# Attention and two MLPs on one core: raw weights fetched earlier and converted from the chunk's first step

## The chip, the core and the metric

The kernel runs on one core of a Trainium2 chip. The metric is the device time of one execution in microseconds (us). Before the change it is 1036.7 us, the median of 3 runs (1035.36 to 1037.4). The core's engines work side by side, each through its own instructions in order, and wait for each other by semaphores: TensorE (PE, with its weight loads PEld), VectorE (DVE), ScalarE (ACT), GpSimd (POOL) and SyncE (SP), which issues the DMAs.

## The reference

```python
def _attn_ref(q, k, v, w1, b1, w2):          # q, k, v: [4, 8, 576, 64]
    ...
    scores = scale * np.matmul(q, k.transpose(0, 1, 3, 2)) + bias.transpose(2, 0, 1)[None, :, :, :]
    ...
    return np.matmul(attn, v)                # attn: softmax of the scores

def _moe_ref(x, w_in, w_out):                # x: [2304, 512], w_in: [512, 2048], w_out: [2048, 512]
    h = x @ w_in
    g = h - np.tanh(h)
    return g @ w_out

def _moe2_ref(x, w_in, w_out, s, b):
    h = x @ w_in
    r = np.maximum(h, 0.0)
    return (s * (r * r) + b) @ w_out

def reference(**kwargs):
    ...
    return _moe2_ref(x=_moe_ref(x=x, **moe_kwargs), **moe2_kwargs)   # x: attn_out as 2304 tokens
```

The weights of both MLPs come as 64-bit floats, so the kernel has to turn each into 32-bit ones, in two parts (a rounded one and what it leaves), before TensorE can use them.

## The kernel before, in words

The program is written in the order in which each engine runs it; no scheduler changes it. Attention goes over 16 pairs of heads in 80 periods (numbered n, with a tail to n = 85). Then comes the **chunk** (`CHUNKS`): 512 tokens of the first MLP with its 16 slices f of the hidden dimension, one per step n = 0 to 15. Then come the super-blocks (`SUPER`), where a product is made of 7 smaller ones: unit sums of the tokens (`tokens`, made in pieces that stand in `xq`) times sums of the weights (`load_w`, `combine`, `part`). The block has 8 pairs p of slices.

A step n of the chunk issues `gemm1(n)` (12 matmuls, h = x times the slice's w_in), `gate(n)` (tanh on ACT, a subtraction on DVE) and `gemm2(n - 2)` (12 matmuls with the slice's w_out); `split(n - 1)` (ACT rounds g, DVE takes the rest) stands ahead of `gemm1(n)`. h lies in one of two PSUM buffers, so `gemm1(n)` writes the one that `split(n - 2)` was the last to read. The products of slices 0 and 1 are made in attention's tail (`PR`).

Between these stands the **conversion** of the 32 half slices of weights, numbered k in the order of the list `wq`: (f, 0) is slice f of w_in, (f, 1) of w_out. `fetch(k)` brings 512 KB of raw weights; conversion k is then `begin(k)` (POOL takes the sign, ACT the value y), `high(k)` and `low(k)` (two DVE operations, the second writes the 32-bit weight x) and `both(k)` (ACT rounds x, POOL takes the rest, and a DMA writes x to `win_d` when it is a w_in, or the two parts to `wsp_d` when it is a w_out):

```python
    def begin(k, raw):
        ...
        x, sg = place(f"s{(0, 1, 6)[k % 3] if k < 32 else (0, 1, 6, 4, 5)[k % 5]}", [512]), place(f"s{2 + k % 2}", [512])
        y = ypool[0].tile([128, 512], F32, tag="y", name="y") if ypool else x
    ...
    def weights_tick():
        a, b_, c = wdone
        if c < b_:
            both(c)
            wdone[2] += 1
        if b_ < a:
            high(b_)
            low(b_)
            wdone[1] += 1
        if a in raw_w:
            begin(a, raw_w.pop(a))
            wdone[0] += 1
```

So x of conversion k lies in one of three buffers, and `low(k)` (line 155) waits until the DMA of `win_d` that reads x of conversion k - 3 has landed, where there is one. y has two PSUM buffers, so `begin(k)` on ACT (line 145) waits for `low(k - 2)`. A tick of the chunk is `both(c)`, `high` and `low` of c + 2 and `begin(c + 3)`. Attention converts k = 0 to 7 in its periods (`TK`), and issues 11 fetches (`FT`, k = 0 to 10); its tail begins conversions 8 to 10. At the chunk's start 8 are done. The number of finished conversions that a step wants is 8 + 2 (n - 2), so steps 0 and 1 have one tick each (a rule of their own), 2 and 3 none, and from step 4 on there are two in each. `fetch_more` then issues the fetches of up to 7 conversions ahead. All these DMAs go through SP, whose issues stand in program order.

Lines that the following speaks of: 372 `gemm1`, 380 and 381 `gate`, 388 and 389 `split`, 613 `gemm2`, 117 `fetch`, 144 and 145 `begin`, 150 `high`, 155 `low`, 161 and 100 `both`, 167 and 176 its DMAs, 775 and 778 the token units, 730 `combine`, 738 and 100 `part`, 920 the super-block's products.

Of the kernel before, what the change touches and what calls it, by code (L numbers as in the profile page):

```python
# [30 lines left out]
RATE = 2.0  # L31
# [13 lines left out]

FT = {1: 0, **{4 + 4 * k: k for k in range(1, 11)}}
ND = 8
TK = {}  # L50
for j, n in enumerate(sorted([41, *range(9, 80, 5)])):
# [15 lines left out]
def tile_kernel(ctx, tc, qk, vd, wcat, wts, sb, ltab, psib, ipsi8, out):  # L67
# [35 lines left out]
    wt, wc_t = {}, {}  # L103

    wq = [(0, 0), (1, 0), (0, 1), (2, 0), (1, 1), (3, 0), (2, 1), (3, 1), (4, 0)]
    wq += [(5 + j // 2 - j % 2, j % 2) for j in range(22)] + [(15, 1)]
    wx_t, wdone = {}, [0, 0, 0]

    raw_w = {}
# [68 lines left out]
# [13 lines that stand above are left out]
# [42 lines left out]
    with ExitStack() as c0:  # L233
# [62 lines left out]
        for n in range(NG + 2):  # L296
            if n < NG:
# [3 lines left out]
                for g in range(4 * G, 4 * G + 4):  # L301
                    hid = hids[g] = hp_.tile([128, LW], F32, tag="h", name="hid")
                    k = min(range(2), key=lambda k: held[k] + HC[k][0] + HC[k][1] * nd)
# [88 lines left out]
    with ExitStack() as ca:  # L392
# [15 lines left out]
        load, hi, lo = load_x(0)  # L408
# [190 lines left out]
    with ExitStack() as cb:  # L599
# [61 lines left out]
        j = 0  # L661
        for P in range(1, 16):
            q, p = divmod(P, 8)
# [47 lines left out]
        def load_w(q, p):  # L711
            if p >= NF // 2:
                q, p = q + 1, p - NF // 2
            if q < len(SUPER):
                if (q, p) not in wf_t:
                    wf_t[q, p] = place(f"w{4 - p}" if q == 0 and p < 2 else f"st{(p + 1) % 2}", [2, 512])
                nc.sync.dma_start(out=wf_t[q, p], in_=win_d[SUPER[q][0], 2 * p:2 * p + 2].rearrange("f p n -> p f n"))
# [37 lines left out]
        def tokens(q):  # L755

            layer, c0, hw = SUPER[q]
            kept = {}

            def raw(kk, half):  # L760
                return kept[kk][:, half * hw:half * hw + hw]

            def load(*kks):
                if q and 0 not in kept:
                    c = place(f"C{(q + 1) % 2}", [4096])
                    for kk in range(4):
                        kept[kk] = c[:, 2 * hw * kk:2 * hw * kk + 2 * hw]
                for kk in kks:
                    if not q:
                        kept[kk] = place(f"w{5 + kk}", [2 * hw])  # L770
                    nc.sync.dma_start(out=kept[kk], in_=source(layer, kk, c0, 2 * hw))

            def hi(u, *xs):
                for i, x in enumerate(xs):
                    nc.scalar.copy(unit(q, u, i, 0), x)

            def lo(u, i, x):
                nc.vector.tensor_tensor(out=unit(q, u, i, 1), in0=x, in1=unit(q, u, i, 0).bitcast(F32), op=ALU.subtract)  # L778

            def minus(o, a, b):  # L780
                nc.vector.tensor_tensor(out=o, in0=a, in1=b, op=ALU.subtract)

            def los(u, *xs):
                for i, x in enumerate(xs):
                    lo(u, i, x)

            def first(i):
                lo(0, i, raw(i, 0))
                minus(raw(i, 0), raw(i, 1), raw(i, 0))

            def third(i):
                minus(raw(i, 0), raw(2 + i, 0), raw(i, 0))
                minus(raw(i, 1), raw(2 + i, 1), raw(i, 1))

            def both(k, h):
                return [raw(k + i, h) for i in range(2)]

            return [lambda: load(0, 1), lambda: load(2, 3),
                    lambda: hi(0, *both(0, 0)), lambda: first(0), lambda: (first(1), hi(3, *both(0, 0))), lambda: los(3, *both(0, 0)),
                    lambda: ([minus(raw(i, 0), raw(2 + i, 1), raw(i, 0)) for i in range(2)], hi(1, *both(0, 0))),  # L800
                    lambda: los(1, *both(0, 0)), lambda: third(0), lambda: (third(1), hi(2, *both(0, 1))),
                    lambda: los(2, *both(0, 1)), lambda: hi(4, *both(2, 0)), lambda: (los(4, *both(2, 0)), hi(5, *both(0, 0))),
                    lambda: (los(5, *both(0, 0)), hi(6, *both(2, 1))), lambda: los(6, *both(2, 1))]

        g_at = {}

# [36 lines left out]
        xq = tokens(0)  # L843
        xq.insert(3, xq.pop(1))
        for n in range(NS):
            want = min(32, ND + max(0, int(RATE * (n - 2))))
            if n < 2:
                weights_tick()
            last = [seq[n - 1]] if len(PR) < n <= len(seq) else []
            if n > 12:  # L850
                split(*last.pop())
            while wdone[2] < want:
                weights_tick()
                if last:
                    split(*last.pop())
            if last:
                split(*last.pop())
            fetch_more(AHEAD)
            c, f = seq[n]
            if n >= len(PR):  # L860
                gemm1(c, f)
                gate(c, f)
            if n >= LAG:
                gemm2(*seq[n - LAG])
            for _ in range({8: 1, 9: 2, 10: 2, 11: 1, 12: 1, 13: 1, 14: 1, 15: 2}.get(n, 0)):
                xq.pop(0)()
            if n == 6:
                load_w(0, 0)
            if n == 9:
                combine(0, 0)  # L870
            if n == 11:
                part(0, 0)
                load_w(0, 1)
            if n == 14:
                combine(0, 1)
        flush(9)
        for _ in range(3):
            n, f, x, _ = back.pop(0)
# [1 line left out]
            wt[f, 1] = place(f"w{x}", [2, 512], F32R)  # L880
            nc.sync.dma_start(out=wt[f, 1].bitcast(F32), in_=wsp_d[f])
        split(*seq[-1])
        while len(xq) > 3:
            xq.pop(0)()

        h_ctx.close()
        ypool.clear()
# [6 lines left out]
        for q, (layer, c0, hw) in enumerate(SUPER):  # L894
# [30 lines left out]
            for p in range(NF // 2):  # L925
                keeps(q, p, "S")
                X, Y, Z, V = (bank(t, hw) for t in ("XYZV", "YXZV")[p % 2])
                load_w(q, p + 2)
                u2, r, t_x = (ring(F32)[:, 0:hw] for _ in range(3))
                product(X, p, 4, 0, True)  # L930
                nc.scalar.copy(u2, X)
                if p + 1 < NF // 2:
                    part(q, p + 1)
                product(Y, p, 0, 1, True)
                nc.vector.tensor_tensor(out=u2, in0=Y, in1=u2, op=ALU.add)
                product(Z, p, 1, 2, True)
                nc.vector.tensor_tensor(out=r, in0=Z, in1=u2, op=ALU.add)
                product(V, p, 2, 3, True)
                nc.vector.tensor_tensor(out=Y, in0=V, in1=r, op=ALU.add)  # L939
                if q == p == 0:  # L940
                    xq.pop(0)()
                if pend:
                    second_products(0, 2 * p - 2, pend.pop(0))
                elif fill:
                    fill.pop(0)()
                squashed(layer, Y, r)
                units(layer, held_unit(layer, 2 * p + 1), Y, r)
                if q == p == 0:
                    xq.pop(0)()
                    xq.pop(0)()  # L950
                keeps(q, p, "A")
                product(X, p, 5, 4, False)
                squashed(layer, X, t_x)
                units(layer, X, X, t_x)
                product(Z, p, 6, 5, False)
                nc.vector.tensor_tensor(out=Z, in0=Z, in1=u2, op=ALU.add)
                g1 = two(hw)
                upper(layer, X, g1)
                t_z = ring(F32)[:, 0:hw]
                squashed(layer, Z, t_z)  # L960
                lower(layer, X, g1)
                units(layer, Z, Z, t_z)
                product(V, p, 3, 6, False)
                nc.vector.tensor_tensor(out=V, in0=V, in1=u2, op=ALU.add)
                g2 = two(hw)
                upper(layer, Z, g2)
                lower(layer, Z, g2)
                squashed(layer, V, t_z)
                units(layer, held_unit(layer, 2 * p), V, t_z)
                if pend:  # L970
                    second_products(0, 2 * p - 1, pend.pop(0))
                elif fill:
                    fill.pop(0)()
                pend = [g1, g2]
                if p + 1 < NF // 2:
                    combine(q, p + 2)
                keeps(q, p, "E")
                if q == FIRST1 and p + 1 < NF // 2:
                    for f in (2 * p + 2, 2 * p + 3):
                        renewed(f)  # L980
                if p == NF // 2 - 1 and not final:
                    xq = tokens(q + 1)
                    for _ in range(3):
                        xq.pop(0)()
# [104 lines left out]
```

## Time and profile before

| | |
|---|---|
| median of 3 runs | 1036.7 us |
| the profiled execution | 1036.71 us, its span 1034.9 us |
| PE, PEld, DVE, ACT, POOL busy | 99%, 80%, 71%, 56%, 56% of the span |
| DMA | 170.47 MB, mean 165 GB/s |
| chain that ended last | PE 85%, DVE 4%, DMA 2%, POOL 2% |

The span runs from the first to the last instruction of the profiled execution; the time has 1.8 us around it. Attention lies at about 50 to 282 us of the span, the chunk's steps at about 280 to 358 us, and the super-blocks follow. Busy shares are means over all of these; what one stage costs is read from that stage.

### The profile page before, as it was taken

The numbers are of one execution on the slowest core, as the hardware profiler recorded it, in microseconds if no ns is written. First come the engines' busy times: TensorE is split into PE (matmuls) and PEld (weight loads), VectorE is DVE, ScalarE is ACT, GpSimd is POOL, SyncE is SP. The second block draws the span as 40 slices with busy tenths as digits, with TensorE's granted clock in tenths as the row PEclk, the third lists the DMA queues.
The fourth block names the chain that finished last, engine by engine and source line by source line (L and its number), as shares of the span: only waits on it lengthen the run. The fifth ranks groups of instructions, "written<-read, shape, count | busy, mean of one in ns | idle before, by whom it ended". The sixth has DMA issues, their size and how long they took to land.

```text
span 1034.9 us, 18742 instructions
## 1 busy us (share of the span) xinstructions
PE 1023.1 (99%) x6664; PEld 832.1 (80%) x6664; DVE 738.3 (71%) x1495; ACT 584.1 (56%) x1208; POOL 577.6 (56%) x706
## 2 busy tenths in 40 slices
PE   9999999999999999999999999999999999999998
PEld 4366666666688789999788888999989998899986
DVE  8899999998668787887777776455575556655551
ACT  8887778777556565544545444455544444454441
POOL 3266666677558678850776631498515664076400
PEclk9999999999999999999999999999999999999999
DMA  7857666554199667867677548411202112031000
GB/s 282 321 178 243 202 214 206 175 176 124 58 360 337 256 223 269 279 218 253 214 242 246 203 146 313 132 62 41 90 23 92 41 61 92 1 96 58 1 31 30
DMA packets 68348, 170.47 MB, mean 165 GB/s; under 512 B 7456, under 2 KB 13728, under 8 KB 68256
## 3 DMA queue, kind: packets, MB, share of 16 engines
q1 hardware_dynamic: 67824, 168.89, 47.2%
q8 instruction: 52, 0.85, 0.3%
q10 hardware_dynamic: 432, 0.39, 0.1%
q14 instruction: 40, 0.33, 0.1%
HBM read 123.22 MB, written 46.04 MB: 164 GB/s over the span
## 4 chain that ended last, share of the span: by engine, by line
PE 85%; DVE 4%; DMA 2%; POOL 2%; ACT 1%; issue 1%; SPq 0%; DVEq 0%; ACTq 0%; POOLq 0%
PE a L613 22%; PE o L536 8%; PE Z L920 8%; PE V L920 8%; PE s L437 7%; PE Y L920 6%; PE X L920 5%; PE V L613 5%; PE Z L613 5%; PE t L481 3%; PE h L372 2%; PE X L613 2%; PE Y L613 2%; PE c L481 1%; DMA w<-x_d 1%
## 5 line engine op out<-in xcount | busy, mean ns | idle before, releaser
L100 POOL TENSOR_TENSOR C<-st,C 128x512 fp32r<-128x512 f32 x76 | 76.4, 1028 | 172.1 <-ACT C L738 133.0
L475 POOL TENSOR_SCALAR pn<-p,sm 128x576 f32<-128x576 f32 (+2 forms) x224 | 132.6, 609 | 61.6 <-DVE sm L466 36.0
L613 PE MATMUL a<-w,ring 128*128 128x512 f32 x576 | 146.5, 392 | 0.0
L613 PE MATMUL a<-ring,w 128*128 128x512 f32 (+1 forms) x576 | 127.5, 371 | 0.0
L613 PEld LDWEIGHTS a<-w,ring 128*128 128x128 f32 x576 | 107.5, 188 | 20.5
L613 PEld LDWEIGHTS a<-ring,w 128*128 128x128 f32 x576 | 105.5, 188 | 14.9
L458 ACT ACTIVATE p<-raw,mn 128x576 f32<-128x576 f32 x144 | 110.9, 773 | 5.0 <-DVE mn L444 2.2
L100 POOL TENSOR_TENSOR C<-XB,C 128x512 fp32r<-128x512 f32 x80 | 108.3, 1376 | 0.0
L444 DVE CUSTOM_DVE_ANT_0 raw<-s,bias 128x576 f32<-128x576 f32 x144 | 103.6, 751 | 4.8 <-PE s L437 4.3
L920 PE MATMUL Z<-C,C 128*128 128x384 f32 (+1 forms) x480 | 102.6, 347 | 1.9 <-DVE C L778 0.8
L536 PE MATMUL o<-pt,vv 128*64 128x256 f32 (+1 forms) x640 | 95.0, 418 | 0.3 <-DVE xo L543 0.2
L437 PE MATMUL s<-qk 64*128 64x288 f32 (+1 forms) x640 | 91.5, 429 | 1.0 <-DVE mn L444 1.0
L920 PEld LDWEIGHTS Z<-C,C 128*128 128x128 f32 x480 | 85.2, 188 | 8.2 <-DVE C L778 2.1
L437 PEld LDWEIGHTS s<-qk 64*128 64x128 f32 (+1 forms) x640 | 47.0, 175 | 41.4 <-issue 18.3
L144 POOL TENSOR_SCALAR s<-w 128x512 f32<-128x512 f32 x60 | 48.2, 807 | 51.9 <-DVE s L150 25.4
L730 POOL TENSOR_TENSOR XB<-st 128x256 f32<-128x256 f32 x76 | 61.3, 807 | 14.5 <-DMA st<-win_d 12.3
L519 ACT COPY pt<-t 128x512 f32<-128x512 f32 x64 | 37.3, 583 | 44.5 <-PE c L481 29.5
L815 ACT ACTIVATE ring<-Y 128x384 f32<-128x384 f32 (+1 forms) x40 | 20.5, 513 | 73.9 <-PE Y L920 42.2
L815 ACT ACTIVATE ring<-X 128x384 f32<-128x384 f32 (+1 forms) x40 | 20.5, 513 | 71.0 <-DVE X L939 37.2
L481 PEld LDWEIGHTS t<-ident,pn 64*128 64x128 f32 x1184 | 51.7, 139 | 7.6 <-issue 0.6
L536 PEld LDWEIGHTS o<-pt,vv 128*64 128x64 f32 x640 | 38.9, 136 | 22.9 <-DVE xo L543 0.5
L481 PE MATMUL t<-ident,pn 64*128 64x64 f32 x1184 | 54.2, 223 | 0.0
(167 smaller groups left out, 2270.1 us busy)
## 6 DMA issues: line engine op xcount, KB each, us to landing
w<-in_wts SPq DMA_DIRECT2D x60, 512.0 KB, 4.8
w<-wsp_d SPq DMA_DIRECT2D x47, 512.0 KB, 4.9
st<-win_d SPq DMA_DIRECT2D x38, 512.0 KB, 3.9
qk<-in_qk SPq DMA_DIRECT2D x16, 864.0 KB, 6.1
bias_d<-m SPq DMA_DIRECT2D x36, 296.0 KB, 4.0
bias<-bias_d SPq DMA_DIRECT2D x32, 288.0 KB, 5.0
win_d<-s SPq DMA_DIRECT2D x32, 256.0 KB, 5.9
wsp_d<-w SPq DMA_DIRECT2D x16, 512.0 KB, 7.0
```

Source lines behind the costliest of these rows:

```text
L100: nc.gpsimd.tensor_tensor(out=lo, in0=raw, in1=hi.bitcast(F32), op=ALU.subtract)
L144: nc.gpsimd.tensor_scalar(out=sg, in0=hw, scalar1=0.0, scalar2=1.0, op0=ALU.mult, op1=ALU.mult)
L437: nc.tensor.matmul(o[0:n, c, 0:288], q[h, ee, t * 128:t * 128 + n], kk[h, ee], start=True, stop=True)
L444: nc.vector.tensor_tensor_reduce(out=raw.rearrange("p (c j) -> p c j", c=2), in0=s_t.pop((x, j))[:, :, 0:288], in1=bias_t[pairs[i][0], k]. ...
L458: nc.scalar.activation(out=p, in_=raw, func=AF.Exp, scale=-1.0, bias=mn, accum_out=sm[:, j:j + 1])
L475: nc.gpsimd.tensor_scalar(out=pn[:, c:c + b - a], in0=p[:, a:b], scalar1=sm[:, j:j + 1], scalar2=0.0, op0=ALU.mult, op1=ALU.add)
L481: nc.tensor.transpose(out_, in_, ident[ROWS[r], ROWS[r]])
L536: nc.tensor.matmul(o[h], v[:, e, j], unit_t[i, u][:, 8 if j == 4 else 4 * e + j, 0:n], start=(j == 0), stop=(j == 4))
L613: nc.tensor.matmul(o, x, y, start=first and j == 0, stop=last and j == 2)
L730: nc.gpsimd.tensor_tensor(out=o, in0=a, in1=b, op=op)
L815: nc.scalar.activation(out=t, in_=c, func=(AF.Tanh, AF.Relu)[layer])
L920: nc.tensor.matmul(o, cs[:, a, l, i * 128:i * 128 + 128], unit(q, u, i, r), start=begins and i == 0 and j == 0, stop=i == 1 and j == 2, sk ...
```

## The change

The list of the half slices gets another order from the tenth on: w_out of slices 4 to 7 first, then w_in of 6 to 9, then in turns again. Attention fetches three more raws (k = 11, 12, 13) at periods 60, 64 and 68. The chunk's wanted number becomes 8 + max(1, 2 n): one tick in steps 0 and 1, two in each of steps 2 to 12, none after. The token pieces (one more, since one was cut in two) all stand in steps 8 to 15, most of them in 12 to 15; before, four of them stood behind the loop and in the super-block's first pair. `combine(0, 0)` moves from step 9 to 11 and `part(0, 0)` from 11 to 13.

```diff
-FT = {1: 0, **{4 + 4 * k: k for k in range(1, 11)}}
+FT = {1: 0, **{4 + 4 * k: k for k in range(1, 11)}, 60: 11, 64: 12, 68: 13}
...
-    wq += [(5 + j // 2 - j % 2, j % 2) for j in range(22)] + [(15, 1)]
+    wq += [(5, 0), (4, 1), (5, 1), (6, 1), (7, 1), (6, 0), (7, 0), (8, 0), (9, 0)]
+    wq += [(8 + j // 2 + j % 2 * 2, 1 - j % 2) for j in range(12)] + [(14, 1), (15, 1)]
...
-                    lambda: los(2, *both(0, 1)), lambda: hi(4, *both(2, 0)), lambda: (los(4, *both(2, 0)), hi(5, *both(0, 0))),
-                    lambda: (los(5, *both(0, 0)), hi(6, *both(2, 1))), lambda: los(6, *both(2, 1))]
+                    lambda: los(2, *both(0, 1)), lambda: hi(4, *both(2, 0)), lambda: los(4, *both(2, 0)),
+                    lambda: (hi(5, *both(0, 0)), hi(6, *both(2, 1))), lambda: los(5, *both(0, 0)), lambda: los(6, *both(2, 1))]
...
-            want = min(32, ND + max(0, int(RATE * (n - 2))))
-            if n < 2:
-                weights_tick()
+            want = min(32, ND + max(1, int(RATE * n)))
...
-            for _ in range({8: 1, 9: 2, 10: 2, 11: 1, 12: 1, 13: 1, 14: 1, 15: 2}.get(n, 0)):
+            for _ in range({8: 1, 9: 2, 10: 1, 11: 1, 12: 2, 13: 3, 14: 3, 15: 3}.get(n, 0)):
...
-            if n == 9:
+            if n == 11:
                 combine(0, 0)
-            if n == 11:
+                load_w(0, 1)
+            if n == 13:
                 part(0, 0)
-                load_w(0, 1)
...
-        while len(xq) > 3:
-            xq.pop(0)()
...
-                if q == p == 0:
-                    xq.pop(0)()
...
-                if q == p == 0:
-                    xq.pop(0)()
-                    xq.pop(0)()
```

**SP at the chunk's start.** The rows `in_wts` are fetches, `wsp_d<-w` and `win_d<-s` are outputs of conversions; `win_d<-s_5025` before and `win_d<-s_5031` in the change are the same one, of conversion 9. Before:

```order
L176 DMA wsp_d<-w_4474 128x1024
L167 DMA win_d<-s_4995 128x512
L117 DMA w_5076<-in_wts 128x512
L117 DMA w_5078<-in_wts 128x512
L117 DMA w_5080<-in_wts 128x512
L117 DMA w_5082<-in_wts 128x512
L117 DMA w_5084<-in_wts 128x512
L117 DMA w_5086<-in_wts 128x512
L117 DMA w_5088<-in_wts 128x512
L176 DMA wsp_d<-w_4968 128x1024
L167 DMA win_d<-s_5025 128x512
```

And SP in the change, at the same place (its lines are one higher):

```order
L177 DMA wsp_d<-w_4480 128x1024
L168 DMA win_d<-s_5001 128x512
L118 DMA w_5087<-in_wts 128x512
L118 DMA w_5089<-in_wts 128x512
L118 DMA w_5091<-in_wts 128x512
L118 DMA w_5093<-in_wts 128x512
L177 DMA wsp_d<-w_4974 128x1024
L168 DMA win_d<-s_5031 128x512
L118 DMA w_5106<-in_wts 128x512
```

Four fetches in place of seven stand ahead of the output of conversion 9.

**DVE at the chunk's start.** `h<-h,ring` is a gate's subtraction, `ring<-h,ring` a split's; the pairs `y<-y,s` and `s<-w,y` are `high` and `low`. Before, from `low(10)` on (`s_5170` is written by `low(12)`, in the buffer of `s_5025`):

```order
L155 SCALAR_TENSOR_TENSOR s_5048<-w_3069,y 128x512
L381 TENSOR_TENSOR h<-h,ring 128x512
L389 TENSOR_TENSOR ring<-h,ring 128x512
L381 TENSOR_TENSOR h<-h,ring 128x512
L150 SCALAR_TENSOR_TENSOR y<-y,s_5095 128x512
L155 SCALAR_TENSOR_TENSOR s_5094<-w_5076,y 128x512
L389 TENSOR_TENSOR ring<-h,ring 128x512
L150 SCALAR_TENSOR_TENSOR y<-y,s_5171 128x512
L155 SCALAR_TENSOR_TENSOR s_5170<-w_5078,y 128x512
```

And DVE in the change, from the same place (`s_5101` is written by `low(12)`, in the buffer of `s_5031`):

```order
L156 SCALAR_TENSOR_TENSOR s_5054<-w_3069,y 128x512
L151 SCALAR_TENSOR_TENSOR y<-y,s_5083 128x512
L156 SCALAR_TENSOR_TENSOR s_5082<-w_3900,y 128x512
L151 SCALAR_TENSOR_TENSOR y<-y,s_5102 128x512
L156 SCALAR_TENSOR_TENSOR s_5101<-w_4114,y 128x512
L151 SCALAR_TENSOR_TENSOR y<-y,s_5114 128x512
L156 SCALAR_TENSOR_TENSOR s_5113<-w_4318,y 128x512
L382 TENSOR_TENSOR h<-h,ring 128x512
L151 SCALAR_TENSOR_TENSOR y<-y,s_5124 128x512
L156 SCALAR_TENSOR_TENSOR s_5123<-w_5087,y 128x512
L390 TENSOR_TENSOR ring<-h,ring 128x512
```

`low(12)` stood behind the gate and split of slice 2 and the split of slice 3; now it stands ahead of the gate of slice 2.

**ACT at the same place**, in the change (`y<-w` is `begin`, `C<-s` and `w<-s` are `both`, `ring<-h` a gate's tanh and, as CAST, a split):

```order
L146 ACTIVATE y<-w_4318 128x512
L162 CAST w_5118<-s_5082 128x512
L146 ACTIVATE y<-w_5087 128x512
L381 ACTIVATE ring<-h 128x512
L162 CAST w_5166<-s_5101 128x512
L146 ACTIVATE y<-w_5089 128x512
L389 CAST ring<-h 128x512
```

The tanh of slice 2 (the first row `ring<-h`) now has `begin(14)` (`y<-w_5087`) right ahead of it.

## Rows read from the trace of the kernel before

**Rows 1.** The page's first part: busy time, share of the span, instructions.

```profile
PE 1023.1 (99%) x6664; PEld 832.1 (80%) x6664; DVE 738.3 (71%) x1495; ACT 584.1 (56%) x1208; POOL 577.6 (56%) x706
```

**Rows 2.** Busy time by stretch: length, five engines, granted clock, DMA share, GB/s.

```profile
290.00:298.00 8.00, 8.00 (x37) 6.62 (x36) 2.88 (x6) 2.74 (x5) 3.82 (x4) 1.00 1.00 368
```

**Rows 3.** Timeline of SP at the chunk's start: start, length, line, DMA, count.

```profile
282.08 3.92 SPq L117 DMA_DIRECT2D w<-in_wts  x7
286.10 0.41 SPq L176 DMA_DIRECT2D wsp_d<-w  x1
286.61 5.33 SPq L167 DMA_DIRECT2D win_d<-s  x2
```

**Rows 4.** DMA issues, us to landing: at 282.1, 284.1, 285.6 and 286.6 us.

```profile
w<-in_wts SPq DMA_DIRECT2D x1, 512.0 KB, 4.3
...
w<-in_wts SPq DMA_DIRECT2D x1, 512.0 KB, 6.5
...
w<-in_wts SPq DMA_DIRECT2D x1, 512.0 KB, 9.9
...
win_d<-s SPq DMA_DIRECT2D x1, 256.0 KB, 11.2
```

**Rows 5.** Timeline of DVE, steps 2 to 4; in brackets idle time and releaser.

```profile
287.61 0.70 DVE L381 TENSOR_TENSOR h<-h,ring 128x512 f32<-128x512 f32 x1 [4.28 <-ACT ring L380]
...
290.17 0.69 DVE L150 SCALAR_TENSOR_TENSOR y<-y,s 128x512 int32<-128x512 int32 x1
290.90 0.69 DVE L155 SCALAR_TENSOR_TENSOR s<-w,y 128x512 int32<-128x512 int32 x1
291.50 0.68 DVE L389 TENSOR_TENSOR ring<-h,ring 128x512 fp32r<-128x512 f32 x1
...
297.88 0.69 DVE L155 SCALAR_TENSOR_TENSOR s<-w,y 128x512 int32<-128x512 int32 x1 [5.09 <-issue]
```

**Rows 6.** Timeline of ACT, steps 2 to 5.

```profile
287.00 0.58 ACT L380 ACTIVATE ring<-h 128x512 f32<-128x512 f32 x1
...
298.68 0.62 ACT L161 CAST w<-s 128x512 fp32r<-128x512 f32 x1 [4.62 <-DVE s L155]
...
299.78 0.58 ACT L388 CAST ring<-h 128x512 fp32r<-128x512 f32 x1
```

**Rows 7.** Timeline of PE: steps 4, 12 and 14, and the super-block's first pairs.

```profile
290.54 2.88 PE L372 MATMUL h<-X,C 128*128 128x512 f32 x12
...
334.06 2.88 PE L372 MATMUL h<-X,C 128*128 128x512 f32 x12
...
346.88 3.03 PE L372 MATMUL h<-X,C 128*128 128x512 f32 x12 [1.34 <-DVE ring L389]
...
373.92 1.23 PE L920 MATMUL Y<-XA,C 128*128 128x384 f32 x6
374.99 1.20 PE L920 MATMUL X<-w,C 128*128 128x384 f32 x6
```

**Rows 8.** Timeline of DVE, the split ahead of step 14's products.

```profile
346.14 0.69 DVE L389 TENSOR_TENSOR ring<-h,ring 128x512 fp32r<-128x512 f32 x1 [1.06 <-ACT ring L388]
```

**Rows 9.** Timeline of POOL, `part(0, 0)` at step 11.

```profile
335.08 2.32 POOL L100 TENSOR_TENSOR C<-w,C 128x512 fp32r<-128x512 f32 x2
337.37 2.85 POOL L100 TENSOR_TENSOR C<-XB,C 128x512 fp32r<-128x512 f32 x2
```

**Rows 10.** Busy time by stretch behind PE's last work (columns as in rows 2).

```profile
1031.10:1036.20 5.10, 0.00 (x0) 0.00 (x0) 0.42 (x1) 0.37 (x1) 0.00 (x0) 1.00 0.17 57
1036.40:1036.90 0.50, 0.00 (x0) 0.00 (x0) 0.00 (x0) 0.00 (x0) 0.00 (x0) 0.50 0.00 0
```

**Rows 11.** PE's first weight loads, and those of `gemm2`: ns, min/median/max, first and last start.

```profile
L242 PEld LDWEIGHTS b<-ident x16: 288/333/333, 1.4 to 4.5; 128*128 128x128 f32 x16
...
L613 PEld LDWEIGHTS a<-ring,w x126: 187/188/188, 299.8 to 357.5; 128*128 128x128 f32 x126
```

**Rows 12.** All outputs to `win_d`, 270 to 380 us: issue to landing.

```profile
DMA to landing us min/median/max: 2.1/6.6/11.2
```

## The prediction

> **What bounds the kernel now.** I read the page first, then the stretches, then the timelines of all engines from 280 to 375 us, where the change lies. PE is busy for 1023.1 us of a span of 1034.9 [rows 1], so less than 12 us can be won by any change that leaves PE's work as it is, and a wait of PE is paid in full unless a later one shrinks by it. In the chunk PE takes no rest: from step 4 at 290.54 to step 12 at 334.06 lie 16 groups of 12 matmuls in 43.52 us, 2.72 us each [rows 7]. The conversions hide beside that, but not with much room: in steps 4 and 5 the DMA queues are busy all the time, at 368 GB/s [rows 2].
>
> Two places matter. At the end PE waits. Step 14's products start at 346.88, after 1.34 us of idleness, since the split before them ran on DVE at 346.14 [rows 7, 8]; ahead of that POOL's `part(0, 0)` stood between the ticks for 5.1 us [rows 9]. Further waits follow in the super-block's first pair. The whole stretch, from step 12 at 334.06 to the second pair at 373.92, takes 39.9 us [rows 7]. Its work is 8 groups of the chunk and two groups that were left for the pair, 10 x 2.72 = 27.2 us, and seven products of 1.07 us (from the pair's first to its second product [rows 7]), 7.5 us: 34.7 us. So 5.2 us are waits.
>
> At the start nothing on PE shows, but DVE shows how near a wait is. `low(12)` starts at 297.88 after 5.09 us of idleness without a named releaser [rows 5]. The output of conversion 9, which reads the same buffer, was issued at 286.61 [rows 3] and took 11.2 us [rows 4]: it landed at 297.8, and that is the releaser. It took so long because seven fetches and a `wsp_d` output were issued ahead of it [rows 3]. The fetches land in their order of issue: the first at 282.1 + 4.3 = 286.4, the fourth at 284.1 + 6.5 = 290.6, the seventh at 285.6 + 9.9 = 295.5 [rows 4], one per 1.4 to 1.6 us; the two outputs behind them take 2.3 us more.
>
> **The change part by part.**
>
> *Three fetches in attention, two ticks from step 2.* The order of DVE shows `low(12)` now ahead of the gate of slice 2; before it stood two steps later. Its wait is the same, for the output of conversion 9. On SP that output now stands behind four fetches and the `wsp_d` output. So it lands at 290.6 + 2.3 = 292.9 us, 4.9 us earlier than before, but it is now wanted two steps, 10.9 us, earlier. Call the landing T. What queues behind it on DVE and ACT, with the distances that rows show:
> - `low(12)` starts at T + 0.1 (297.88 behind 297.8 [rows 5]); ACT, which waits for it, starts 0.8 us after it (298.68 [rows 6]), at T + 0.9. That is `begin(14)`, which needs the y buffer of `low(12)`.
> - The tanh of slice 2 stands right behind `begin(14)` on ACT: two ACT operations take 298.68 to 299.78, 0.55 each [rows 6], so T + 1.45. DVE's subtraction follows a tanh by 0.6 (287.00 [rows 6] to 287.61 [rows 5]): T + 2.05.
> - `high(14)`, `low(14)` and the split of slice 2 follow on DVE, at distances of 0.6, 0.7 and 0.6 (`high` at 290.17, `low` at 290.90, a split at 291.50 [rows 5]; 0.6 for the first): the split starts at T + 3.95.
> - PE's next products start 0.74 after the split that they wait for (346.14 [rows 8] to 346.88 [rows 7]): T + 4.7.
>
> Those products are `gemm1(4)`, which writes the h buffer of slice 2. It starts at 292.9 + 4.7 = 297.6 in place of 290.54 [rows 7], and PE has nothing else to do: **+7.1 us**. Bounds for T: 291.3, if the two outputs need only the 0.7 us of one of half the size behind the last fetch (worked out from 1.4 us per fetch), and 294.5, if every fetch takes the 1.6 us of the last three [rows 4]; so +5.5 to +8.7. I take 292.9, since it takes all its parts from the same queue in the same state.
>
> After this wait the conversions are ahead again. The next wait on such an output is `low(17)` on conversion 14. By the same distances it delays the split of slice 4 to about 1 us before PE wants it, because PE itself is later; I count 0, and at most +3.
>
> *The clock of TensorE.* It is 1.00 at the chunk's start [rows 2], and the rest of 1.34 us ahead of step 14 [rows 7] is the longest that PE takes in the chunk. Behind PE's last work it is 1.00 up to 1036.2 and 0.50, the lower of the two levels, from 1036.4 [rows 10], after some 5 us of rest. A rest of 7.1 us is longer, so I let the clock fall. Low weight loads are seen at the program's start: 333 ns, against 188 later, over 16 matmuls from 1.4 to 4.5 us [rows 11]. If `gemm1(4)` and what follows run for as long, 3.8 us, at half the speed, 1.9 us are lost: **+1.9 us**, with 0 (the clock holds) and 2.7 (a whole group at half speed) as bounds. The Trainium skill ("TensorE: Matmul & The Clock Gate", section "HAM oscillation — how this bites in real kernels") says that a wait for DMA of several us lets the clock fall to half, and that the matmuls behind it begin at the slow level. By the kernel's own work alone, in which no row shows a fall, this term would be 0 and the sum +2.5; by the rule it is a loss of half of the throttled time, and the sum that of the forecast or a little more. The rows behind PE's last work agree with the rule; no row of the trace before shows it in mid kernel.
>
> *The end of the chunk.* Ticks end at step 12, `part(0, 0)` comes after them, and no token piece is left for the first pair. So the waits of 5.2 us go, but something takes their place: step 13 now has six DVE operations of tokens between a gate and a split, and on ACT two token roundings and the three of `part` ahead of the split's. Reckoned in the same way, this split comes 0.4 us too late for `gemm1(15)`, and the fourth product of the first pair, whose bank is that of slice 15, waits some 0.2 us. So **-4.6 us**, at best -5.2, at worst -3.
>
> *The fetches in attention* cost three SP issues of 0.6 us (seven in 3.92 [rows 3]) and 1.5 MB in a time when the queues are not full; attention's own loads are issued periods ahead. I count 0, at most +0.5. The other order of `wq` costs nothing by itself: w_in of slice 6 is done in step 3 and wanted in step 6.
>
> The sum: 7.1 + 1.9 - 4.6 = +4.4. The profiled execution took 1036.71 us, as the median, so 1041.1 us.
>
> **The rivals.**
> - *The output lands early* (faster). Outputs of this kind land 2.1 us after issue at best [rows 12]. If conversion 9's did, issued at about 285.0 (four fetches of 0.56 us and the `wsp_d` output behind 282.08 [rows 3]), T would be 287.1 and `gemm1(4)` would start at 291.8: 1.3 us lost, no rest long enough for the clock, and 4.6 won, 1033.4 us. The point from which it decides is T = 290.4, where wait and gain are equal. Against it: the same output landed behind all seven fetches, and these in order [rows 4]. For it there is a rule: the Trainium skill ("DMA: Bandwidth & Descriptors", section "Queues, rings and completion order") says that completion is not first in, first out for an issuing engine. In this trace's rows at this place it was.
> - *The clock holds* at a wait of 5.5 to 7.1 us: 1037.6 to 1039.2, half of it no change that can be measured.
> - *The outputs chain* (slower still). Conversions 14 to 17 are four w_in in a row now, so `low(17)` to `low(20)` each wait for an output. If the queue is 2 us later than I reckon, PE rests a second time, 3 us: 1044 us.
>
> **How the numbers follow.** Wait and low clock: 0.58. The clock holds: 0.18, a third of it within the bound and the rest above. The output lands early: 0.12. The chain: 0.12. About 0.2%, 2.1 us, is what a measurement of this kernel tells from no change. Below 1034.6 lies the early landing, 0.12; within the bound a third of the second case and the lower end of the first, 0.14; the rest, 0.74, is slower. The range must reach from the case in which the clock holds and T is early, 1037.6, to the chain, 1044; it leaves out the early landing and little else.
>
> **What would show it.** Right: PE idle for about 7 us ahead of `gemm1(4)`, near 290.5, released by a split on DVE; `low(12)` on DVE idle up to about 292.9, until conversion 9's output lands; a granted clock below 1.00 in the 4 us behind; steps 12 to 15 and the first pair without waits over 0.5 us, 35.3 us from step 12 to the second pair. Wrong: an output of conversion 9 that lands before 290.4, a PE that rests less than 4 us there, or a stretch from step 12 to the second pair that stays near 39.9 us.

## The result and the profile after

The changed kernel takes 1044.15 us, the kernel before 1037.05 us in the runs beside it: a ratio of 1.0066, 95% interval 1.0051 to 1.0082. The profiled execution took 1044.29 us (span 1042.5), 7.58 us more than that of before. One run of 1664.57 us, at a granted clock of 0.556, was a disturbed one: the ratio leaves it out, the median counts it (without it, it is 1044.02).

The timeline of PE in the changed kernel, to be read beside [rows 7]; the columns are start, length, line, operation, count, and in brackets idle time and releaser. 299.42 is `gemm1(4)`, 341.38 `gemm1(11)`, 346.95 step 12, 381.76 the second pair:

```profile
288.17 2.88 PE L614 MATMUL a<-ring,w 128*128 128x512 f32 x12
299.42 4.86 PE L373 MATMUL h<-X,C 128*128 128x512 f32 x12 [8.37 <-DVE ring L390]
304.12 2.91 PE L614 MATMUL a<-ring,w 128*128 128x512 f32 x12
...
336.78 2.88 PE L614 MATMUL a<-ring,w 128*128 128x512 f32 x12
341.38 3.02 PE L373 MATMUL h<-X,C 128*128 128x512 f32 x12 [1.72 <-DVE ring L390]
...
346.95 2.88 PE L373 MATMUL h<-X,C 128*128 128x512 f32 x12
...
381.76 1.23 PE L917 MATMUL Y<-XA,C 128*128 128x384 f32 x6
```

The same place by stretch (length, PE, PEld, DVE, ACT, POOL, granted clock, DMA share, GB/s), as [rows 2]:

```profile
290.90:293.00 2.10, 0.15 (x1) 0.00 (x0) 0.00 (x0) 0.00 (x0) 0.00 (x0) 1.00 1.01 407
293.00:294.50 1.50, 0.00 (x0) 0.00 (x0) 0.00 (x0) 0.00 (x0) 0.00 (x0) 0.55 1.07 433
294.60:299.40 4.80, 0.00 (x0) 0.00 (x0) 4.51 (x8) 3.81 (x8) 2.13 (x3) 0.50 1.03 420
299.50:304.10 4.60, 4.60 (x12) 3.62 (x13) 4.26 (x7) 3.34 (x6) 4.60 (x5) 0.58 1.00 350
```

From 291.1 to 294.5 no engine works: everything stands, and only the DMA queues run. Then DVE and ACT work off what had queued, and PE starts last, at the lower of its two levels of clock. DVE and ACT of the changed kernel show what all waited for, as [rows 5] and [rows 6] did:

```profile
294.82 0.69 DVE L156 SCALAR_TENSOR_TENSOR s<-w,y 128x512 int32<-128x512 int32 x1 [7.83 <-DMA win_d<-s]
295.42 0.69 DVE L151 SCALAR_TENSOR_TENSOR y<-y,s 128x512 int32<-128x512 int32 x1
296.15 0.69 DVE L156 SCALAR_TENSOR_TENSOR s<-w,y 128x512 int32<-128x512 int32 x1
296.75 0.69 DVE L382 TENSOR_TENSOR h<-h,ring 128x512 f32<-128x512 f32 x1
...
298.07 0.69 DVE L156 SCALAR_TENSOR_TENSOR s<-w,y 128x512 int32<-128x512 int32 x1
298.68 0.68 DVE L390 TENSOR_TENSOR ring<-h,ring 128x512 fp32r<-128x512 f32 x1
...
340.04 0.69 DVE L156 SCALAR_TENSOR_TENSOR s<-w,y 128x512 int32<-128x512 int32 x1 [0.53 <-DMA win_d<-s]
```

```profile
295.54 0.63 ACT L146 ACTIVATE y<-w 128x512 f32<-128x512 f32 x1 [7.95 <-DVE s L156]
296.10 0.58 ACT L381 ACTIVATE ring<-h 128x512 f32<-128x512 f32 x1
...
337.14 0.51 ACT L776 CAST XA<-w 128x384 fp32r<-128x384 f32 x1 [5.00 <-DMA w<-x_d]
```

The first line of each is `low(12)` and `begin(14)`; on DVE `high(13)` and `low(13)` follow, then the subtraction of slice 2 at 296.75, `low(14)` at 298.07 and the split of slice 2. The releaser is now named, the DMA that writes conversion 9's x to `win_d`. SP had issued it at 285.60, behind four fetches and a `wsp_d` output, as [rows 3] with fewer fetches:

```profile
282.43 2.44 SPq L118 DMA_DIRECT2D w<-in_wts  x4
284.92 0.62 SPq L177 DMA_DIRECT2D wsp_d<-w  x1
285.60 0.57 SPq L168 DMA_DIRECT2D win_d<-s  x1
```

The DMA issues of the changed kernel, as [rows 4]: the first of the four fetches, the output, and the tokens' first load, issued at 328.6 (KB each, us to landing):

```profile
w<-in_wts SPq DMA_DIRECT2D x1, 512.0 KB, 5.2
...
win_d<-s SPq DMA_DIRECT2D x1, 256.0 KB, 9.1
...
w<-x_d SPq DMA_DIRECT2D x1, 384.0 KB, 8.5
```

So the balance of the changed kernel against before, up to the second pair (381.76 against 373.92, +7.84), is: chunk begun 0.35 later; rest ahead of `gemm1(4)` 8.53 (299.42 - 288.17 - 2.72); that group 4.70 long instead of 2.72, +1.98; rest ahead of `gemm1(11)` 1.88; from step 12 to the second pair 34.81 instead of 39.86, -5.05. The sum is +7.7 of the 7.84 (the group at 341.38 took 2.85 us, 0.13 more than 2.72), and later stretches differ by 0.3 us in all.

### The profile page after: what moved, and what is told of

Read it like the earlier page. It is cut to its first block, busy times and chain, and to the rows that moved or that the text cites. A ratio compares the mean times of both kernels' runs of the same rounds, so it can differ in the third digit from the quotient of the medians.

```text
span 1042.5 us, 18794 instructions
## 1 busy us (share of the span) xinstructions
PE 1023.4 (98%) x6664; PEld 834.1 (80%) x6664; DVE 735.7 (71%) x1495; ACT 584.9 (56%) x1208; POOL 574.4 (55%) x706
## 4 chain that ended last, share of the span: by engine, by line
PE 88%; DMA 4%; DVE 3%; issue 2%; POOL 2%; ACT 1%; SPq 0%; POOLq 0%; DVEq 0%; ACTq 0%
PE a L614 23%; PE Z L917 8%; PE V L917 8%; PE o L537 8%; PE s L438 7%; PE Y L917 6%; PE X L917 6%; PE V L614 5%; PE Z L614 5%; PE t L482 3%; PE h L373 3%; DMA win_d<-s 2%; PE Y L614 2%; PE X L614 2%; POOL m L286 1%
## 5 line engine op out<-in xcount | busy, mean ns | idle before, releaser
L373 PE MATMUL h<-X,C 128*128 128x512 f32 x192 | 48.8, 405 | 10.1 <-DVE ring L390 10.1
```

The lines of the kernel that those rows point to most:

```text
L373: nc.tensor.matmul(h, a, x, start=(k == 0), stop=(k == 3 * KD - 1))
```

## The experiments

Eleven kernels were run, in four groups, each beside runs of the kernel before on the same chip. Its medians there were 1036.17, 1036.02, 1036.37 and 1036.23 us.

**1. Five buffers x in plain turn.** Conversion 12 no longer writes the buffer of conversion 9.

```diff
-        x, sg = place(f"s{(0, 1, 6)[k % 3] if k < 32 else ...
+        x, sg = place(f"s{(0, 1, 6)[k % 3] if k < 8 else (6, 0, 1, 4, 5)[(k - 8) % 5] if k < 32 else ...
```

> The changed kernel with five buffers x in turn for conversions 8 to 31 instead of three, so that the low half of conversion 12 no longer writes the buffer that conversion 9's output is read from. Theory (the wait ahead of gemm1(4) is the wait for that buffer): gemm1(4) starts at 291 to 292 us instead of 299.4, what then ends last being raw 14, which landed at 287.6, with the same chain of 4 us behind it; the 2.0 us of slow clock behind the rest go too, so 1033 to 1036 us against 1044.2. Whether the 1.9 us ahead of gemm1(11) go as well decides inside that range. Rival (two conversions per step are more than ScalarE, VectorE and GpSimd do in a step, whichever buffer they write): gemm1(4) starts later than 296 us and the time stays above 1041 us. Rival (the fetches themselves are late, so the conversions wait for raw words instead): gemm1(4) starts at 294 to 298 us, 1039 to 1042 us.

Measured: 1039.51 us, ratio 1.0029 (1.0019 to 1.0039). Faster than the change by some 4 us, and the rest ahead of `gemm1(11)` is gone (it starts at 336.10, right behind its forerunner). But PE still waits at the old place, until 296.37:

```profile
296.37 4.51 PE L373 MATMUL h<-X,C 128*128 128x512 f32 x12 [5.29 <-DVE ring L390]
```

DVE shows why:

```profile
288.22 0.69 DVE L156 SCALAR_TENSOR_TENSOR s<-w,y 128x512 int32<-128x512 int32 x1
288.95 0.70 DVE L382 TENSOR_TENSOR h<-h,ring 128x512 f32<-128x512 f32 x1
289.56 0.69 DVE L151 SCALAR_TENSOR_TENSOR y<-y,s 128x512 int32<-128x512 int32 x1
295.02 0.69 DVE L156 SCALAR_TENSOR_TENSOR s<-w,y 128x512 int32<-128x512 int32 x1 [4.77 <-issue]
295.63 0.68 DVE L390 TENSOR_TENSOR ring<-h,ring 128x512 fp32r<-128x512 f32 x1
```

`low(13)` runs at 288.22 and the subtraction of slice 2 at 288.95, 7.8 us earlier than in the change. But with five in plain turn the buffer of conversion 9 comes back at conversion 14, and `low(14)`, right ahead of the split of slice 2 on DVE, now waits for the same output, which landed at 294.9. The third theory's numbers fit (294 to 298 us, 1039 to 1042 us), but only by luck, since its mechanism doesn't: `begin(14)` ran at 287.77, as soon as raw 14 was there. The first named the right output and forgot which conversion would be next to want its buffer.

**2. No fetches in the chunk's first step.** Three buffers as in the change; conversion 9's output goes first.

```diff
-            fetch_more(AHEAD)
+            if n:
+                fetch_more(AHEAD)
```

> The changed kernel without the fetches that the chunk's first step issues (they follow in the second step), so that conversion 9's output is queued ahead of all of them. Three buffers x as before. Theory (the output is late because four fetches of 512 KB stand ahead of it in the queue): it lands at 286 to 288 us instead of 294.7, gemm1(4) starts at 291 to 294 us, where raw 14, now issued later, ends last; 1034 to 1038 us. Rival (the output is late by its own transfer, or by the conversion that makes it): it lands later than 292 us all the same and the time stays at 1042 to 1045 us.

Measured: 1040.16 us, ratio 1.0040 (1.0023 to 1.0056). In the DMA issues the output, now issued at 284.2, takes

```profile
win_d<-s SPq DMA_DIRECT2D x1, 256.0 KB, 4.1
```

and lands at 288.3: the four fetches ahead of it were what made it late. What ends last is now raw 14, issued behind it: ACT waits for it until 290.85, and PE rests 2.68 us:

```profile
294.70 4.58 PE L373 MATMUL h<-X,C 128*128 128x512 f32 x12 [2.68 <-DVE ring L390]
```

`gemm1(4)` comes 0.7 us later than expected, no more than the 0.97 by which this chunk began later than the change's. The time is 2 us above the expectation: the clock fell all the same (below), and `gemm1(6)` waited another 1.74.

**3. The pace of before, all else as changed.**

```diff
-            want = min(32, ND + max(1, int(RATE * n)))
+            want = min(32, ND + max(0, int(RATE * (n - 2))))
+            if n < 2:
+                weights_tick()
```

> The changed kernel with the pace of conversions of the kernel before (one per step in the first two steps, two per step from the fifth), all else as changed: the three early fetches, the order of the weights, and the token pieces, combine and part in the later steps. Theory: conversion 12's low half is back in step 4, as in the kernel before, and gemm1(4) starts at 290.9 to 291.5 us with no fall of the clock; but the conversions now end in the steps that also have two to three token pieces each, so the 5 us of waits at the end of the chunk come back, 5 to 9 us of them; 1036 to 1041 us. Rival (the 5 us were gained by moving the token pieces alone): 1031 to 1033 us. Rival (the early step's loss comes from the three early fetches or the order of the weights, not from the pace): gemm1(4) starts later than 296 us, 1043 us or more.

Measured: 1041.63 us, ratio 1.0047 (1.0030 to 1.0064), 0.6 us over the expectation. No wait at step 4, so the early loss belongs to the pace. The loss at the end is back and larger. On PE `gemm1(15)`, and on ACT what stands ahead of its split:

```profile
358.86 5.49 PE L373 MATMUL h<-X,C 128*128 128x512 f32 x12 [4.47 <-DVE ring L390]
```

```profile
354.38 0.51 ACT L776 CAST C<-w 128x384 fp32r<-128x384 f32 x1 [4.39 <-DVE w L782]
355.31 0.51 ACT L776 CAST C<-w 128x384 fp32r<-128x384 f32 x1 [0.43 <-DVE w L782]
355.73 0.92 ACT L739 CAST C<-w 128x512 fp32r<-128x512 f32 x2
356.56 1.04 ACT L739 CAST C<-XB 128x1024 fp32r<-128x1024 f32 x1
357.50 0.57 ACT L389 CAST ring<-h 128x512 fp32r<-128x512 f32 x1
```

Token roundings and `part` stand ahead of the split in steps that still convert. At the old pace, moving the pieces does not win the 5 us; the kernel loses as much against the one before.

**4. The kernel before with five buffers** (the first edit, on the kernel before).

> The kernel before with five buffers x in turn for conversions 8 to 31 instead of three, nothing else. Theory: there the wait for conversion 9's output (VectorE idle 5.09 us at 297.9) ended beside PE's work and cost nothing, and the waits at the end of the chunk come from tokens, combine and part standing among the conversions; so the same time within 1 us, 1036 to 1038 us. Rival (three buffers slow the conversions through the whole chunk, so that the end of it is late): 2 to 5 us faster, 1032 to 1035 us, with fewer waits ahead of the gemm1 of steps 13 to 15.

Measured: 1036.11 us, ratio 0.9997 (0.9987 to 1.0006). The buffer is no bound at the pace of before, as expected; the wait of [rows 5] was covered. Its chunk also began at 279.87, without early fetches: the 0.35 us of the change are no cost of theirs that a run shows (across these kernels, alike up to there but for the fetches, it began at 279.1 to 280.8).

**5. Five buffers given out late.** As the first run, but by a list, so that conversion 9's buffer comes back at conversion 17.

```diff
+XB = (6, 0, 1, 4, 5, 1, 4, 6, 5, 0, 1, 4, 1, 6, 5, 1, 0, 5, 4, 0, 6, 4, 1, 6)
...
-        x, sg = place(f"s{(0, 1, 6)[k % 3] if k < 32 else ...
+        x, sg = place(f"s{XB[k - 8] if 8 <= k < 32 else (0, 1, 6)[k % 3] if k < 8 else ...
```

> The changed kernel with five buffers x as before this run, but given out by a list, so that the buffer of a conversion whose output goes to memory comes back latest: conversion 9's next at conversion 17 (with five in plain turn it came back at 14, where VectorE waited 4.77 us for the same output, which landed at 294.9 us). Theory (that one output is the whole of the early wait): begin(14) runs at 287.8 us as with five in plain turn, its split is done at 291 us, gemm1(4) starts at 291.3 to 292.0 us without a fall of the clock behind it; against the 1039.5 us of five in plain turn that takes off 4.5 us of rest and 1.6 us of slow clock: 1033.4 us, 1032.5 to 1034.5. Rival (another late transfer stands right behind: raw words 16 and 17 landed at 291.8 and 293.3 us there): gemm1(4) or gemm1(5) still waits 2 us or more, 1036 to 1039 us.

Measured: 1036.27 us, ratio 1.0004 (0.9995 to 1.0013): no difference from before. PE's timeline:

```profile
291.98 3.01 PE L374 MATMUL h<-X,C 128*128 128x512 f32 x12 [0.63 <-DVE ring L391]
...
309.42 3.02 PE L374 MATMUL h<-X,C 128*128 128x512 f32 x12 [0.83 <-DVE ring L391]
...
332.94 3.02 PE L374 MATMUL h<-X,C 128*128 128x512 f32 x12 [1.47 <-DVE ring L391]
...
355.33 3.03 PE L374 MATMUL h<-X,C 128*128 128x512 f32 x12 [0.32 <-DVE ring L391]
```

The early wait is gone but for 0.63 us, and the clock holds: that output was its cause. What is left hangs on raw 14, for which `begin(14)` on ACT waited 1.60 us, until 288.12. But of the 6.1 us expected against the first run 3.2 came. Waits that the late PE had covered stand up: `gemm1(7)`, behind a `low` that waits 5.16 us for an output, and `gemm1(11)`, behind ACT's wait of 5.16 us for the tokens' load. The stretch from 282 to 318 us suggests what is short:

```profile
282.00:318.00 36.00, 34.53 (x152) 27.95 (x151) 28.52 (x45) 24.21 (x44) 29.47 (x32) 1.00 1.02 381
```

No engine but PE is near full, DMA is. But it was full before, too (a share of 1.00, 366 GB/s, with PE at 36.00), so the share alone proves nothing; that two conversions per step ask for more than the queue carries is put to the test in run 9.

**6. The same with tokens, `combine` and `part` in their old places** (fetches, order and pace as changed).

> The same five buffers given out by a list, the early fetches, the order of the weights and the new pace, but the token pieces, combine and part in the places of the kernel before (steps 8 to 15, part of them behind the chunk). Theory (pace and places are both needed for the end of the chunk: with the old pace and the new places it lost 6.7 us): the waits ahead of the gemm1 of steps 13 to 15 go, since the conversions are over by step 12, but the pieces behind the chunk still hold the first pair, by the 1 to 2 us of waits seen there before; 1033.5 to 1036 us. Rival (the pace alone ends the chunk early): the same time as with the new places within 0.5 us. Rival (the places are what counts): 1037 us or more.

Measured: 1037.25 us, ratio 1.0013 (1.0004 to 1.0022), 1.0 us above the run before. In the chunk PE's waits are as long (3.5 us against 3.3), and the first pair takes 1.1 us more between two `gemm2` groups. PE of this run, then of run 5:

```profile
365.19 2.92 PE L615 MATMUL a<-ring,w 128*128 128x512 f32 x12
...
372.20 2.92 PE L615 MATMUL a<-ring,w 128*128 128x512 f32 x12
```

```profile
365.11 2.92 PE L615 MATMUL a<-ring,w 128*128 128x512 f32 x12
...
371.02 2.92 PE L615 MATMUL a<-ring,w 128*128 128x512 f32 x12
```

So about 1 of the 5 us at the end comes from the places of the pieces, and the rest from the pace, with conversions over by step 12. (The new order of the weights goes with the pace in these runs; none parts the two.) The absolute time was 1.2 us over what I had expected, because run 5 was.

**7. The same without the early fetches.**

```diff
-FT = {1: 0, **{4 + 4 * k: k for k in range(1, 11)}, 60: 11, 64: 12, 68: 13}
+FT = {1: 0, **{4 + 4 * k: k for k in range(1, 11)}}
```

> The same five buffers given out by a list, and all of the change, but without the three early fetches in attention: raw words 11 to 17 are then all fetched at the chunk's start, seven in a row. Theory (a conversion cannot begin before its raw words land, and these land one after the other): raw 14 is fourth in the row and lands at 291 to 293 us instead of 287.7, begin(14) waits for it and gemm1(4) starts at 295 to 297 us, with 1.7 to 2 us of slow clock behind it; 1038 to 1041 us. Rival (the raw words are early enough anyway): 1033 to 1034 us, the same as with the early fetches.

Measured: 1037.87 us, ratio 1.0010 (0.9999 to 1.0020). PE rested 4.24 us and `gemm1(4)` started at 294.87, as expected (the time is just below what I had put), though by raw 11 (`begin(11)` on ACT waited 5.08 us for it) and not by raw 14. Yet the time is only 1.6 us above run 5: behind this wait no other followed, since a late PE again covers the waits of steps 7 and 11. The profile overstates this run's loss: the profiled execution, at 1039.3, was the slowest of ten.

**8 and 9. Tokens one to two steps later, and a smoother pace.** Run 8 is run 5 with the first pair of lines, run 9 has both pairs:

```diff
-            for _ in range({8: 1, 9: 2, 10: 1, 11: 1, 12: 2, 13: 3, 14: 3, 15: 3}.get(n, 0)):
+            for _ in range({8: 1, 10: 2, 11: 2, 12: 2, 13: 3, 14: 3, 15: 3}.get(n, 0)):
...
-            want = min(32, ND + max(1, int(RATE * n)))
+            want = min(32, ND + max(1, int(1.85 * n)))
```

> Five buffers x given out by the list, and the first token cast (hi(0)) in step 10 instead of step 9, the second load of tokens in step 11 instead of 9. With the buffers alone, ScalarE waited 5.16 us for the tokens, which landed 8.3 us after their issue behind the raw words, and gemm1(11) then waited 1.47 us. Theory (that wait is the token load standing behind the raw fetches in the one queue, and the cast standing ahead of split(9) on ScalarE): the cast no longer waits, the wait ahead of gemm1(11) goes, 1.6 us off: 1034.0 to 1035.5 us. Rival (the queue is full, so the lateness only moves to the next load): a wait of 1 us or more at gemm1(11) to gemm1(14), 1035.8 to 1037 us.

> As the run before, and the pace 1.85 conversions per step instead of 2, which with rounding down puts most conversions about half a step to a step later and the last in step 13. Theory (two conversions per step from the first step ask for more transfers than the queue carries beside PE at full speed: with the list of buffers its engines were busy 99% of 282 to 318 us, and VectorE waited 5.16 us at 306.1 for an output to leave its buffer): the waits of 0.63 us ahead of gemm1(4) and 0.83 us ahead of gemm1(7) go and nothing new comes at the end, 1.5 us off again: 1032.5 to 1034.5 us. Rival (what is gained early is lost late, as with the old pace and the new places): waits of 1.5 us or more ahead of gemm1(13) to gemm1(15), 1035 to 1038 us.

Measured: 1033.29 us, ratio 0.9969 (0.9958 to 0.9980), and 1032.57 us, ratio 0.9965 (0.9952 to 0.9977). Both beat both kernels. PE of run 8 waits twice in the chunk, no longer ahead of `gemm1(11)`, and that of run 9 once, at its last products:

```profile
290.73 3.02 PE L374 MATMUL h<-X,C 128*128 128x512 f32 x12 [0.43 <-DVE ring L391]
...
308.35 3.02 PE L374 MATMUL h<-X,C 128*128 128x512 f32 x12 [1.00 <-DVE ring L391]
```

```profile
351.61 3.06 PE L374 MATMUL h<-X,C 128*128 128x512 f32 x12 [1.41 <-DVE ring L391]
```

Run 8 is better than expected by 0.7 us; 1 us of its profile is a chunk that began at 279.1, which the edit doesn't touch. Run 9's gain over run 8 isn't distinguishable (the intervals overlap): the two early waits go with the slower pace, as expected, and 1.4 us come back at step 15, close to what the rival had said.

**10. The change with the tokens later, three buffers.** The first pair of lines of the last diff, on the changed kernel.

> The changed kernel with its three buffers x, and only the tokens moved: first cast in step 10, second load in step 11. Theory (the wait of 1.72 us ahead of gemm1(11) is ScalarE's wait for the tokens at 337.1 us): that wait goes and nothing else, gemm1(4) still starts at 299 us; 1042.0 to 1042.8 us against 1044.2. Rival (gemm1(11) is late because the conversions are late since step 4): 1043.8 to 1044.6 us.

Measured: 1045.4 us, ratio 1.0092 (1.0075 to 1.0109): no gain at all. My theory of the wait ahead of `gemm1(11)` fell. ACT no longer waits for the tokens, and DVE waits instead:

```profile
341.15 0.69 DVE L156 SCALAR_TENSOR_TENSOR s<-w,y 128x512 int32<-128x512 int32 x1 [7.01 <-DMA win_d<-s]
```

In the change the same output landed 1.1 us earlier, at 339.9, as the `low` at 340.04 shows, hidden behind the tokens' wait. Both transfers stood in the same queue; with three buffers, taking one wait away left the other. It came out even worse than the rival had it, at 1045.4 for 1043.8 to 1044.6 us, since PE's rest grew and the clock fell behind it too:

```profile
342.50 4.62 PE L373 MATMUL h<-X,C 128*128 128x512 f32 x12 [2.33 <-DVE ring L390]
```

That this rest hangs on the three buffers fits run 1, which has five, the tokens in the change's places, and no rest at `gemm1(11)`.

**11. The best run's pace and token places, three buffers.**

> The best run's pace (1.85 per step) and token places, but the change's three buffers x. Theory (the early loss hangs on conversion 12's low half standing ahead of tanh(2)'s subtraction and split(2) while conversion 9's output is on its way, and 1.85 only moves it from the first to the second tick of step 2): gemm1(4) still starts at 298 to 300 us with the clock falling behind it, 1041 to 1044 us. Rival (the slower pace alone gives the output time to leave): gemm1(4) starts before 292 us, 1032 to 1034 us.

Measured: 1045.29 us, ratio 1.0091 (1.0076 to 1.0106). PE:

```profile
298.25 5.23 PE L373 MATMUL h<-X,C 128*128 128x512 f32 x12 [6.71 <-DVE ring L390]
...
363.62 4.62 PE L373 MATMUL h<-X,C 128*128 128x512 f32 x12 [2.95 <-DVE ring L390]
```

`gemm1(4)` is as late as expected; a rest of 2.95 us ahead of `gemm1(15)`, which I had not expected, puts the time a little above. The buffers alone part this kernel from run 9, by 12.7 us between the medians: there they decide.

## Why the prediction was right

The forecast was 1041.1 us, within 1037.0 to 1044.5 (its outer cases lay at 1037.6 and 1044), and slower at 0.74. Slower it was, with 1044.15 near the upper end: the sum of +4.4 came out as 7.6 in the profiled execution. Term by term:

- **The wait at `gemm1(4)`: mechanism right, 1.4 us too small.** Forecast +7.1 (bounds 5.5 to 8.7), measured 8.53. The length of the chain behind the landing was exact: from T = 294.72 (issued at 285.6, 9.1 us to landing) `gemm1(4)` came at T + 4.70, as forecast. In part that is luck: the forecast left out `high(13)` and `low(13)`, which DVE ran ahead of the subtraction. Their way (296.15 + 0.6 = 296.75) is as long as the one through `begin(14)` and the tanh on ACT (296.10 + 0.6), so the trace doesn't tell which of the two held the subtraction. T itself was put at 292.9. Of the 1.8 us missing, 0.35 is the later start; the rest is the queue: the first fetch took 5.2 us instead of the 4.3 that the row of before gave, and the output landed 7.1 us after that, where 1.4 us per fetch and 2.3 for the outputs made 6.5. What made these longer no run shows. Even my upper bound for T was 0.2 short. Runs 1, 2 and 5 show the cause of the wait: without the fetches ahead the output takes 4.1 us, and with its buffer wanted late enough the rest shrinks to 0.63.
- **The clock: right that it fell, lucky in the size.** Forecast +1.9, measured +1.98, with a granted clock of 0.50 at the end of the rest and 0.58 over the group behind. The Trainium skill ("TensorE: Matmul & The Clock Gate", section "HAM oscillation — how this bites in real kernels") says that matmuls behind such a DMA wait begin at the slow level; the trace agrees. But the 3.8 us that the forecast halved were those of PE's first 16 matmuls, whose weight loads were slow [rows 11] at a granted clock of 1.00, as the trace of before has it from 0 to 5 us, so the trace does not show that a lowered clock slowed them. In other runs the group behind a rest of 4.2 us or more lost 1.6 to 2.6 us.
- **The end of the chunk: right.** Forecast -4.6, best -5.2, measured -5.05. Runs 3 and 6 part it: the pace brings about 4 even with the old places (in run 6 it is 35.88 us from step 12 at 339.08 to the second pair at 374.96, for 39.86 before), the new places 1 more, and the places without the pace lose.
- **The outputs chain: counted at 0, measured 1.9.** This is the term that I mis-sized most, and the tokens' load stood in no term at all. I followed the outputs as far as `low(17)`, where the waits (2.59 us at most on DVE up to step 8) did reach PE as little as I said. At step 11 PE rested 1.72 us, behind the tokens' load and, as run 10 shows, an output behind that. The rival named a second rest of 3 us and 1044 us, at 0.12; its condition was a queue 2 us later than reckoned, and T was 1.8 us later. The kernel did both, the forecast's wait and a second one of this kind, shorter and later than the rival put it, and its time is the rival's.
- **Attention: +0.35**, inside the 0.5 allowed, and within what such a start differs between kernels that are alike up to there.

The rival on the other side, an output that lands before 290.4, was ruled out as the rows had it: the landings came in the order of issue.

## What to carry to other kernels

When work is moved earlier, follow its buffers back: the last reader of each may be a transfer that is still in the queue, and an in-order engine that waits for it holds everything behind. Give out buffers by when they come free, not in plain turn, and issue what frees a buffer ahead of fetches that are wanted later. And reckon the gain of a removed wait net of the waits that it covered: here some 6 us of rest and slow clock went between runs 1 and 5, and 3.2 us of time.

## What the runs showed of the hardware

What the clock cost behind a rest went less regularly than I had thought. `gemm1` groups of 12 matmuls take 2.72 us to the next group. Behind rests of 1.00 to 1.74 us they took 2.84 to 2.89. Behind 2.33, 2.68 and 2.95 us (runs 10, 2, 11) it was 4.46, 4.42 and 4.46: the clock fell behind rests a third as long as that of the forecast. Behind 4.24 to 8.37 us it was anything from 4.35 to 5.29, without order. In the change the clock was down some 6 us before PE began again; in the first run it stayed up all through a rest of 5.29 us and fell only as PE began:

```profile
291.10:296.30 5.20, 0.00 (x0) 0.00 (x0) 1.28 (x3) 0.56 (x1) 2.15 (x3) 0.99 1.03 417
296.40:300.70 4.30, 4.30 (x12) 3.43 (x13) 4.23 (x7) 3.35 (x6) 3.19 (x3) 0.63 1.03 420
```

So each of the longer rests cost 1.6 to 2.6 us in the group behind it, and up to 0.5 in the next, and its length doesn't tell how much. Nor is it the same in every execution of one kernel: those of run 7 go from 1035.62 us, at a granted clock of 1.000 over the whole, to 1039.3 at 0.997. The other thing is the rate of the queues: while PE rested in the change and in run 1, fetches and outputs together moved 407 to 433 GB/s (381 over the 36 us of run 5). The Trainium skill ("DMA: Bandwidth & Descriptors", section "Where 436 GB/s comes from") puts some 358 GB/s, half of what one HBM stack gives its two cores, as what binds transfers between HBM and SBUF; this kernel runs on one core, and these stretches lie above that figure, so the measurement decides.
